# Decoding a weight tile over two attention pairs instead of one

## The chip, the cores and the metric

The kernel runs on one core of one Trainium2 chip. The metric is the device time of one execution in microseconds (us); it is given as the median of several executions. The engines are named as the profile names them: PE (matrix products; PEld is its weight load), DVE (vector), ACT (activation), POOL (GpSimd) and SP (the queue that issues nearly all DMAs).

## The reference

What has to be computed, in float32, cut to what matters:

```python
# q, k, v: (4, 8, 576, 64)
scores = softmax(causal(q @ k.T / 8))          # per batch and head, 576 x 576
local  = scores @ v
q_p    = elu(q) + 1
mem    = (q_p @ M_prev) / (q_p . z_prev + 1e-6)
x      = g * mem + (1 - g) * local             # g = sigmoid(beta), one per head
x      = x.transpose(0, 2, 1, 3).reshape(2304, 512)
h = x @ w_in;  y = (h * tanh(softplus(h))) @ w_out      # 512 -> 2048 -> 512
out = (((y @ w1) * (y @ w2)) @ w3) @ w_out2             # 512 -> 1024 -> 512
```

## The kernel before

The program is written with a tile framework whose planner places the instructions: it simulates the program with estimated costs and gives each engine its queue in the order in which instructions become ready there, the one written first going first. `tc.issue_after(ins)` adds an order against `ins` for the instructions of the block on the same engine only.

**Attention.** There are 16 pairs of heads (NPAIR; a pair is two heads of one batch), worked on one after the other by the loop at lines 578 to 653, with a 17th pass (p = 16) that finishes the last pair and begins the feed-forward part. Pass p loads pair p + 2 (`load_pair`, `load_v`), takes the scores of pair p in blocks of rows, and transposes, multiplies and stores pair p - 1. In the order of the pass:

- `s_blocks(p, (3,))`, `s_blocks(p, (2,))`, `s_blocks(p, (0, 1))` and `s_last(p)`: the score products on PE into a two-bank PSUM tile psA, the row minima of the negated, masked scores on DVE (`maxed`, L400; the text calls them the maxima, as the names do), the exponentials on ACT (L405). Blocks 0 and 1 are the small blocks. `taken[0]` is the last L400 so far.
- `pt_g(p - 1, ..)`: transposes of pair p - 1's weights on PE (L66) into psF, copied out on ACT (L457).
- `prep(p + 1, ..)`: transposes of the next q and k (L66 into psX, copied by ACT, L320), and qd on POOL (L326).
- `normed(p, ..)`: the scaling of the exponentials (L383, L384 on small tiles, then L388 eight times, four on DVE and four on POOL).
- `pv(p - 1)`: the products with v and the memory (psX and psF), copied as a high part by ACT (L478) and a low part by DVE (`sub`, L79). `split_x[0]` is the last such L79.
- `phi_terms(p + 1)`: L342 on ACT, L343 and L349 on POOL, L344 on DVE; `phi_norm(p)`: L358 to L361 on DVE, L364 on POOL.

psX and psF have two banks each, used in turn. A bank is taken again when its reader is through: the first transposes of a pass (`pt_g(p - 1, 1)`) take the psF bank that L79 of the last `pv` reads.

**Decoding.** Each weight is stored as 64-bit words. A tile of 128 x 512 words is fetched by one DMA of 512 KB (`fetch`, L131, tile draw), decoded by six DVE operations (L110, L111, L114, L117, L120, L121) and a POOL addition (L125) into the tile da, and then split into a high part (L76, POOL) and a low part (L79, POOL) in wqt. All six DVE operations and the three of POOL are over 128 x 512 elements.

Eight tiles, the first quarter of w_in and w_out (`load_quarter(0)`: four of w_in, then four of w_out), are decoded during attention. `fetch_next()` issues a tile's DMA, `begin()` puts its seven operations (the last holds L125, L76 and L79) into the list `parts`, and `drip(n, behind)` writes the next n of them. Before, one tile takes one pass: with begin at p = 4 to 11, L110, L111 and L114 stand behind the small blocks' maxima of pass p, L117 behind the L79 of `pv(p - 1)`, L120 behind the maxima of block 3 of pass p + 1, and L121 with the three POOL operations behind those of block 2. draw and da have two buffers each.

**After attention** the first half of the feed-forward part begins with `h_steps((0, 0))` inside pass 16, which reads the w_in tiles; `emit_x2((0, 0))` reads the w_out tiles, the last of them in the second half of each of its output blocks. Two further tiles are decoded right after the first `split_y` (`run(pre, 2)`, line 781). At the end of attention its pools are closed, and x2 takes the place of the decoder's tiles.

Of the kernel before, what the change touches and what calls it, by code (L numbers as in the profile page):

```python
# [21 lines left out]
def fused_kernel(ctx: ExitStack, tc, q, k, v, M_prev, z_prev, beta, w_in, w_out, w1, w2, w3, w_out2, out):  # L22
# [45 lines left out]
    def in_turn(fn, *args):  # L68

        if not ordered[0]:  # L70
            return fn(*args)
        with tc.issue_after(tail[0]):
            return fn(*args)
# [23 lines left out]
    def decoder(stack, raw, n, w=WN, side="left"):  # L97
        dec.update(pool=stack.enter_context(tc.tile_pool(name="dec", bufs=1, side=side)), raw=raw, n=n, w=w)
# [104 lines left out]
    def ensure_x(b):  # L203
        if b not in xl:
            xl[b] = xp.tile([128, 2, KD, 2 * S], F32R, tag=f"xs{b}", name=f"xt{b}")
# [17 lines left out]


    at = ExitStack()
    decoder(at, 2, 2)
    ap_ = at.enter_context(tc.tile_pool(name="attn", bufs=1))

    ek = ExitStack()
# [1 line left out]
    NPAIR = B * NP  # L231
# [52 lines left out]
    def load_pair(p):  # L284
        b, c = divmod(p, NP)
        h0 = 2 * c
        t = {}
        for nm, src in (("q", q), ("k", k)):
            a = ep.tile([128, NB, 2, D], F32, tag="qk", name="raw", bufs=4)
            go = nc.scalar.dma_start if p == 0 and nm == "k" else dm  # L290
            for e in range(2):
                go(out=a[:, 0:4, e], in_=src[b, h0 + e, 0:512, :].rearrange("(i p) d -> p i d", p=128))
            go(out=a[:, 4], in_=src[b, h0:h0 + 2, S - 128:S, :].rearrange("h p d -> p h d"))
            t[nm] = a
        st[p] = t

    def load_v(p):
        b, c = divmod(p, NP)
        h0 = 2 * c
        a = ap_.tile([128, NB, 2, D], F32, tag="vr", name="raw", bufs=3)  # L300
        st[p]["z"] = ep.tile([128, 2, D], F32, tag="zr", name="zr", bufs=3)
        dm(out=st[p]["z"], in_=z_prev[b, h0:h0 + 2].partition_broadcast(128))
        for e in range(2):
            dm(out=a[:, 0:4, e], in_=v[b, h0 + e, 0:512, :].rearrange("(i p) d -> p i d", p=128))
        for hv in (UP, DN):
            dm(out=a[hv, 4], in_=v[b, h0:h0 + 2, 512:S, :].rearrange("h p d -> p h d"))
        st[p]["v"] = a
# [69 lines left out]
    def normed(p, xs):  # L377

        d = st[p]
        og = ogp[:, p % NP]  # L380
        sl = slice(0, 8) if len(xs) > 1 else slice(8, 9)
        rv = d["sum"][:, sl]
        nc.vector.tensor_scalar(out=rv, in0=rv, scalar1=1e-9, scalar2=None, op0=ALU.add)  # L383
        nc.vector.reciprocal(out=rv, in_=rv)  # L384
        for ib, e in xs:
            s = s4[:, 0:S] if ib == 4 else d["s"][ib, e]
            x = 8 if ib == 4 else 2 * ib + e
            r = (nc.gpsimd if x in ON_POOL else nc.vector).tensor_scalar(  # L388
                out=s, in0=s, scalar1=d["sum"][:, x:x + 1], scalar2=og[:, x:x + 1], op0=ALU.mult, op1=ALU.mult
            )  # L390
            if x in ON_POOL:
                scaled[0] = r.ins

    taken = [None]
    scaled = [None]
    split_x = [None]
# [86 lines left out]
    def h_steps(u):  # L483

        g, n = u
        t = wts[g]
        x = xl[n // 3]
        cs = slice(CH * (n % 3), CH * (n % 3) + CH)
        y = [wps[0].tile([128, 2, CH], F32, tag=f"y{i}", name="y", bufs=1) for i in range(2)]
        hp = []  # L490
        for m in range(KQ):
            j = m - (u == (0, 1))
            if j < 0:
                o = psX()[:, 0:CH]
            else:
                if j % 2 == 0:
                    two = psA()
                o = two[:, j % 2, 0:CH]
            ms = slice(128 * m, 128 * m + 128)
            for kk in range(KD):  # L500
                mm(o, t[:, 0, kk, ms], x[:, 0, kk, cs], kk == 0, False)
                mm(o, t[:, 0, kk, ms], x[:, 1, kk, cs], False, False)
                mm(o, t[:, 1, kk, ms], x[:, 0, kk, cs], False, kk == KD - 1)
            hp.append(o)
            yield
        for m in range(KQ):
            nc.scalar.activation(out=y[m // 2][:, m % 2], in_=hp[m], func=AF.Tanh, scale=0.5)  # L507

        d = wps[0].tile([128, 1], F32, tag="dum", name="dum", bufs=2)
        with ExitStack() as k_:  # L510
            if u == (0, 0):
                k_.enter_context(tc.issue_after(copied[0]))
            first = nc.scalar.activation(out=d, in_=y[1][:, 1, 0:1], func=AF.Sin, scale=0.0)
        with tc.issue_after(first.ins):
            for i in range(2):
                nc.scalar.activation(out=y[i], in_=y[i], func=AF.Arctan, scale=-0.5, bias=half)
        for i in range(2):
            nc.scalar.activation(out=y[i], in_=y[i], func=AF.Sin, scale=-2.0, bias=halfpi)  # L518
            for j in range(2):
                nc.vector.tensor_tensor(out=y[i][:, j], in0=y[i][:, j], in1=hp[2 * i + j], op=ALU.mult)  # L520
        yield y

    def emit_h(u, beside=iter(())):

        for m, y in enumerate(h_steps(u)):
            if m == 1:
                steps(beside, 1)
        return y
# [27 lines left out]
    def fetch_next():  # L556
        for src, done in islice(lq0, 1):
            ahead.append((fetch(src), done))

    def begin():  # L560
        r, done = ahead.pop(0)
        ops, a, flat = decode_ops(r)

        def last():
            ops[6]()
            done(a, flat)

        parts.extend(ops[0:6] + [last])

    def drip(n, behind):  # L570

        with tc.issue_after(behind):
            for op in parts[:n]:
                op()
        del parts[:n]

    pre = predecode()
    for p in range(NPAIR + 1):

        now, old, new = p < NPAIR, p > 0, p + 1 < NPAIR  # L580
        ordered[0] = True
        if old:
            ensure_x((p - 1) // (2 * NP))
        if not now:
            ek.close()
            wps[0] = wk.enter_context(tc.tile_pool(name="wp", bufs=1, side="right"))
            h0 = h_steps((0, 0))
        if p + 2 < NPAIR:
            load_pair(p + 2)
            load_v(p + 2)  # L590
        if 3 <= p < 11:
            fetch_next()
        if now:
            in_turn(s_blocks, p, (3,))
            drip(1, taken[0])
            if p == 1:
                in_turn(trans_phi, 0)
        else:
            normed(p - 1, [(4, None)])
            in_turn(next, h0)  # L600
        if old:
            in_turn(pt_g, p - 1, 1)
            in_turn(pt_g, p - 1, 0)
            if not now:
                in_turn(next, h0)
        else:
            gate_values(b_)
            phi_terms(0)
            in_turn(prep, 1, "q")
        if now:  # L610
            in_turn(s_blocks, p, (2,))
            drip(2, taken[0])
            with tc.issue_after(taken[0]):
                if old:
                    normed(p - 1, [(4, None)])
                phi_norm(p)
        if old:
            in_turn(pt_g, p - 1, 4)
            in_turn(pt_g, p - 1, 2)
            if not now:  # L620
                in_turn(next, h0)
            if new:
                in_turn(prep, p + 1, "q")
            in_turn(pt_g, p - 1, 3)
            if not now:
                in_turn(next, h0)
        else:
            in_turn(prep, 1, "k")
        if now:
            in_turn(s_blocks, p, (0, 1))  # L630
            if 4 <= p < 12:
                begin()
                drip(3, taken[0])
        if old and new:
            in_turn(prep, p + 1, "k")
        if old:
            in_turn(pt_g, p - 1, 5)
            in_turn(pt_g, p - 1, 6)
        if now:
            in_turn(s_last, p)  # L640
            with tc.issue_after(taken[0]):
                normed(p, [(i, e) for e in range(2) for i in range(4)])
        if old:
            in_turn(pv, p - 1)
            drip(1, split_x[0])
        if not now:
            split = split_y((0, 0), next(h0))
            early = {(0, 1): emit_h((0, 1))}
        if new:
            with tc.issue_after(taken[0]):  # L650
                phi_terms(p + 1)
        if now and p > 0:
            in_turn(trans_phi, p)
# [260 lines left out]
```

## Time and profile before

| what | value |
|---|---|
| median of 3 executions | 1000.93 us (1000.35 to 1000.98) |
| the profiled execution | 1000.65 us |
| its span, first to last instruction | 998.9 us |
| PE busy | 966.7 us (97%) |
| DVE busy | 639.1 us (64%) |
| ACT busy | 498.4 us (50%) |
| POOL busy | 331.1 us (33%) |
| granted clock of PE, mean of the span | 1.000 |

The shares are means over stages with different limits. The attention part takes up to about 249 us from the start; the rest is the feed-forward part. In the rows below times are us from the start of the span unless marked ns. In rows of a timeline the first two numbers are the start and the length; square brackets hold the engine's idle time before the instruction, and what ended it.

### The profile page before, as it was taken

Reading aid. Unit: us, or ns where it says so; the run is one execution under the profiler, and the core shown is the slowest. Engines: PE = TensorE matmul, PEld = TensorE weight load, DVE = VectorE, ACT = ScalarE, POOL = GpSimd, SP = SyncE. Lnnn points to the kernel's source line nnn. Section 1 sums busy time; section 2 is a strip of 40 time slices with the busy share of each in tenths; the row PEclk is TensorE's granted clock in tenths of the full one; section 3 lists DMA queues with packets and bytes.
Section 4 is the critical chain, followed back from the end, with each engine's and each line's share of the span. In section 5 each row is a group of like instructions: output and inputs, shape, how many; then the busy total and the mean of one; then the engine's idle time right before and its main releaser. Section 6 shows DMA issues by size and latency. Waiting matters only on the chain.

```text
span 998.9 us, 15097 instructions
## 1 busy us (share of the span) xinstructions
PE 966.7 (97%) x5584; PEld 823.6 (82%) x5584; DVE 639.1 (64%) x1380; ACT 498.4 (50%) x1016; POOL 331.1 (33%) x329
## 2 busy tenths in 40 slices
PE   6999888899999999999999999999999999999998
PEld 3565555567999999999999999998888888888897
DVE  5789999974669888988988587676752121121111
ACT  6888677786755555555555554451241221221112
POOL 5547666742244545544454221112400000000000
PEclk9999999999999999999999999999999999999999
DMA  7534443301222242324332672252220100100001
GB/s 160 135 74 110 98 119 81 81 16 64 65 98 92 88 157 99 121 87 138 115 111 81 234 259 98 74 169 74 69 79 1 42 1 1 43 1 22 22 1 64
DMA packets 95770, 85.93 MB, mean 86 GB/s; under 512 B 68816, under 2 KB 72912, under 8 KB 95696
## 3 DMA queue, kind: packets, MB, share of 16 engines
q1 hardware_dynamic: 94368, 84.63, 27.4%
q8 instruction: 44, 0.72, 0.3%
q10 hardware_dynamic: 1328, 0.33, 0.2%
q14 instruction: 30, 0.25, 0.1%
HBM read 67.64 MB, written 17.30 MB: 85 GB/s over the span
## 4 chain that ended last, share of the span: by engine, by line
PE 63%; DVE 25%; ACT 6%; issue 2%; DMA 2%; SPq 1%; POOL 1%; ACTq 0%; DVEq 0%; POOLq 0%
PE psA L63 34%; PE psX L63 15%; PE psF L63 12%; DVE da L117 3%; DVE s L400 3%; DVE draw L120 3%; DVE da L111 3%; DVE da L114 2%; DVE s L388 2%; DVE da L110 2%; ACT s L405 2%; DVE y L520 2%; DVE draw L121 2%; PE psF L66 1%; DVE gl L79 1%
## 5 line engine op out<-in xcount | busy, mean ns | idle before, releaser
L63 PE MATMUL psA<-xt,wqt 128*128 128x384 f32 x1140 | 206.3, 336 | 1.4 <-DVE y L520 1.0
L125 POOL TENSOR_TENSOR da<-da,draw 128x512 f32<-128x512 f32 x72 | 99.0, 1381 | 311.9 <-DVE draw L121 231.8
L63 PEld LDWEIGHTS psA<-xt,wqt 128*128 128x128 f32 x1140 | 197.7, 188 | 4.4 <-DVE y L520 3.6
L842 DVE TENSOR_TENSOR bs<-bs,psA 128x512 f32<-128x512 f32 (+1 forms) x40 | 25.3, 633 | 170.2 <-ACT bs L841 170.2
L63 PE MATMUL psX<-gh,wqt 128*128 128x384 f32 x480 | 122.3, 335 | 0.0
L63 PE MATMUL psA<-x2h,w12t 128*128 128x512 f32 (+1 forms) x384 | 105.4, 354 | 0.0
L841 ACT COPY bs<-psA 128x512 f32<-128x512 f32 (+1 forms) x40 | 21.8, 544 | 164.4 <-PE psA L63 161.8
L405 ACT ACTIVATE s<-s,acc 128x512 f32<-128x512 f32 (+2 forms) x144 | 85.6, 600 | 19.8 <-DVE acc L400 19.2
L63 PE MATMUL psA<-x2s,w12t 128*128 128x512 f32 x384 | 89.6, 389 | 0.0
L63 PEld LDWEIGHTS psX<-gh,wqt 128*128 128x128 f32 x480 | 86.8, 188 | 0.7
L63 PEld LDWEIGHTS psA<-x2s,w12t 128*128 128x128 f32 x384 | 72.1, 188 | 15.0
L63 PE MATMUL psX<-gl,wqt 128*128 128x384 f32 x240 | 80.2, 335 | 0.0
L400 DVE CUSTOM_DVE_ANT_0 s<-psA,mask 128x512 f32<-128x512 f32 (+2 forms) x144 | 63.4, 477 | 24.4 <-PE psA L63 24.0
L66 PEld LDWEIGHTS psF<-ident,s 128*128 128x128 f32 x400 | 43.1, 141 | 43.5 <-ACT pt L457 17.4
L507 ACT ACTIVATE y<-psA 128x384 f32<-128x384 f32 x95 | 41.6, 491 | 71.6 <-PE psA L63 71.3
L63 PEld LDWEIGHTS psA<-x2h,w12t 128*128 128x128 f32 x384 | 68.5, 189 | 10.3
L66 PE MATMUL psF<-ident,s 128*128 128x128 f32 x400 | 61.1, 283 | 14.4 <-DVE xt L79 7.6
L520 DVE TENSOR_TENSOR y<-y,psA 128x384 f32<-128x384 f32 x95 | 48.1, 547 | 41.2 <-ACT y L518 41.2
L63 PE MATMUL psF<-gh,wqt 128*128 128x384 f32 x288 | 73.0, 334 | 0.0
L457 ACT COPY pt<-psF 128x512 f32<-128x512 f32 (+1 forms) x112 | 59.4, 543 | 19.8 <-PE psF L66 19.8
L388 POOL TENSOR_SCALAR s<-s,sum,ogp 128x128 f32<-128x128 f32 (+1 forms) x64 | 53.1, 840 | 45.9 <-DVE sum L384 43.9
L63 PE MATMUL psA<-room,w12t 128*128 128x512 f32 (+1 forms) x192 | 67.9, 354 | 0.0
(121 smaller groups left out, 1903.6 us busy)
## 6 DMA issues: line engine op xcount, KB each, us to landing
draw<-in_moe_w_dram SPq DMA_DIRECT2D x32, 512.0 KB, 3.7
draw<-in_moe_w_out_dram SPq DMA_DIRECT2D x24, 512.0 KB, 3.6
draw<-in_moe_w_in_dram SPq DMA_DIRECT2D x16, 512.0 KB, 4.4
out_dram<-ob SPq DMA_DIRECT2D x18, 256.0 KB, 2.0
raw<-in_q_dram SPq DMA_DIRECT2D x32, 128.0 KB, 3.4
raw<-in_v_dram SPq DMA_DIRECT2D x32, 128.0 KB, 2.5
o_dram<-draw SPq DMA_DIRECT2D x8, 512.0 KB, 2.8
w_dram<-draw SPq DMA_DIRECT2D x8, 512.0 KB, 2.8
```

The costliest lines, as they stand in the source:

```text
L63: tail[0] = nc.tensor.matmul(o, lhsT=l, rhs=r, start=start, stop=stop).ins
L66: tail[0] = nc.tensor.transpose(o, src, ident).ins
L111: lambda: V.tensor_scalar(out=a, in0=a, scalar1=2.0 ** -15, scalar2=122879.9921875, op0=ALU.max, op1=ALU.min),
L117: lambda: V.scalar_tensor_tensor(out=ai, in0=hw, scalar=-0x40000000, in1=ai, op0=ALU.bitwise_and, op1=ALU.bitwise_or),
L120: lambda: V.tensor_scalar(out=hw, in0=ai, scalar1=-0x800000, scalar2=None, op0=ALU.bitwise_and),
L125: lambda: nc.gpsimd.tensor_tensor(out=a, in0=a, in1=lw.bitcast(F32), op=ALU.add),
L388: r = (nc.gpsimd if x in ON_POOL else nc.vector).tensor_scalar(out=s, in0=s, scalar1=d["sum"][:, x:x + 1], scalar2=og[:, x:x + 1], op0=ALU ...
L400: taken[0] = nc.vector.tensor_tensor_reduce(out=s, in0=o, in1=m, op0=ALU.add, op1=ALU.min, scale=-scale, scalar=init, accum_out=a,).ins
L405: nc.scalar.activation(out=s, in_=s, func=AF.Exp, scale=-1.0, bias=a, accum_out=r)
L457: copied[0] = nc.scalar.copy(out=t[:, 0:n], in_=o[:, 0:n]).ins
L507: nc.scalar.activation(out=y[m // 2][:, m % 2], in_=hp[m], func=AF.Tanh, scale=0.5)
L520: nc.vector.tensor_tensor(out=y[i][:, j], in0=y[i][:, j], in1=hp[2 * i + j], op=ALU.mult)
```

## The change

The eight tiles are spread over all sixteen pairs, and each takes two passes. Tiles are fetched at even p from 0 to 14 and begun at odd p from 1 to 15. In odd passes L110, L111 and L114 follow the small blocks' maxima, and L117 the L79 of `pv(p - 1)`: the places that these four had before. In even passes L120, L121 and the three POOL operations follow the small blocks' maxima; nothing follows the maxima of blocks 3 and 2 any more. The last tile is begun at p = 15 and ends in pass 16, behind `pv(15)`. da has one buffer in place of two.

```diff
-    decoder(at, 2, 2)
+    decoder(at, 2, 1)
...
-        if 3 <= p < 11:
+        if p % 2 == 0 and p < NPAIR:
             fetch_next()
         if now:
             in_turn(s_blocks, p, (3,))
-            drip(1, taken[0])
...
             in_turn(s_blocks, p, (2,))
-            drip(2, taken[0])
...
             in_turn(s_blocks, p, (0, 1))
-            if 4 <= p < 12:
+            if p % 2 == 1:
                 begin()
-                drip(3, taken[0])
+            drip(3, taken[0])
...
             in_turn(pv, p - 1)
-            drip(1, split_x[0])
+            if p % 2 == 1 or not now:
+                drip(3 if not now else 1, split_x[0])
```

## Rows read from the trace of the kernel before

**Rows 1.** Windows: stretch, us, busy PE, PEld, DVE, ACT, POOL; PE clock, DMA share, GB/s.
```profile
69.69:83.34 13.65, 13.21 (x104) 8.27 (x102) 12.80 (x41) 11.66 (x35) 9.27 (x10) 1.00 0.37 93
83.34:98.78 15.44, 13.49 (x104) 8.24 (x102) 15.27 (x43) 11.62 (x35) 10.60 (x12) 1.00 0.44 96
...
177.26:193.09 15.83, 13.56 (x104) 8.25 (x103) 15.27 (x42) 11.60 (x35) 10.98 (x12) 1.00 0.30 69
...
206.73:220.38 13.65, 13.21 (x104) 8.27 (x103) 10.05 (x36) 11.66 (x35) 6.98 (x8) 1.00 0.11 26
```

**Rows 2.** Waits of PE from 83 to 193 us: total us, times, longest.
```profile
PE psF L66 <- DVE xt L79: 7.6, 7, 1.1
PE psF L66 <- DVE s L388: 3.2, 7, 0.5
```

**Rows 3.** Timeline of DVE in the frame at 206.73, which has no decoding.
```profile
207.88 0.82 DVE L344 SCALAR_TENSOR_TENSOR phie<-phie,phit 128x640 f32<-128x640 f32 x1
...
209.05 1.45 DVE L388 TENSOR_SCALAR s<-s,sum,ogp 128x256 f32<-128x256 f32 x4
...
211.33 0.21 DVE L79 TENSOR_TENSOR xt<-psF,xt 128x64 fp32r<-128x64 f32 x1
...
220.58 0.46 DVE L400 CUSTOM_DVE_ANT_0 s<-psA,mask 128x288 f32<-128x288 f32 x1 [1.61 <-PE psA L63]
```

**Rows 4.** Timeline of DVE around 69.69: the first tile, begun in pass 4.
```profile
68.19 0.53 DVE L110 TENSOR_SCALAR da<-draw 128x512 int32<-128x512 int32 x1
...
69.89 0.46 DVE L400 CUSTOM_DVE_ANT_0 s<-psA,mask 128x288 f32<-128x288 f32 x1
...
74.42 0.68 DVE L117 SCALAR_TENSOR_TENSOR da<-draw,da 128x512 int32<-128x512 int32 x1
75.52 0.69 DVE L400 CUSTOM_DVE_ANT_0 s<-psA,mask 128x512 f32<-128x512 f32 x1 [0.41 <-PE psA L63]
```

**Rows 5.** Timelines of POOL and DVE in a later pass with decoding.
```profile
129.34 1.25 POOL L364 TENSOR_TENSOR phie<-phie,dn 128x640 f32<-128x640 f32 x1
...
129.66 1.22 DVE L110 TENSOR_SCALAR da<-draw 128x512 int32<-128x512 int32 x1
```

**Rows 6.** Tile draw up to 240 us: ns shortest/median/longest, first and last start; landing.
```profile
L120 DVE TENSOR_SCALAR draw<-da x8: 801/1300/1680, 76.7 to 185.8; 128x512 int32<-128x512 int32 x8
L121 DVE SCALAR_TENSOR_TENSOR draw<-draw x8: 677/682/690, 78.4 to 188.4; 128x512 f32<-128x512 uint32 x8
...
DMA to landing us min/median/max: 3.5/4.1/6.7
```

**Rows 7.** Tile da over the whole span, its POOL operations: ns shortest/median/longest.
```profile
L125 POOL TENSOR_TENSOR da<-da,draw x72: 1283/1313/1699, 79.2 to 719.5; 128x512 f32<-128x512 f32 x72
...
L76 POOL TENSOR_SCALAR wqt<-da x32: 612/653/829, 81.1 to 551.0; 128x512 fp32r<-128x512 f32 x32
L79 POOL TENSOR_TENSOR wqt<-da,wqt x32: 1277/1312/1453, 83.6 to 551.8; 128x512 fp32r<-128x512 f32 x32
```

**Rows 8.** Timelines of POOL and DVE after the last tile's L121, frame at 193.09.
```profile
193.52 1.28 POOL L79 TENSOR_TENSOR wqt<-da,wqt 128x512 fp32r<-128x512 f32 x1
...
194.23 1.25 DVE L344 SCALAR_TENSOR_TENSOR phie<-phie,phit 128x640 f32<-128x640 f32 x1
...
197.80 0.21 DVE L79 TENSOR_TENSOR xt<-psF,xt 128x64 fp32r<-128x64 f32 x1
```

**Rows 9.** Timeline of PE in the frame at 206.73: the first transposes.
```profile
212.44 1.09 PE L66 MATMUL psF<-ident,s 128*128 128x128 f32 x8
```

**Rows 10.** Timeline of SP near the start: the first load of pair 3.
```profile
19.70 1.09 SPq L292 DMA_DIRECT2D raw<-in_q_dram  x2
```

**Rows 11.** Timelines of DVE and PE after pv(15), as the feed-forward part begins.
```profile
257.42 0.22 DVE L79 TENSOR_TENSOR xt<-psF,xt 128x64 fp32r<-128x64 f32 x1
...
263.15 0.51 PE L63 MATMUL psX<-gh,wqt 128*128 128x384 f32 x2
```

**Rows 12.** Groups of POOL from 60 to 200 us by form: count, busy us, mean ns.
```profile
L388 POOL TENSOR_SCALAR s<-s,sum,ogp 128x512 f32<-128x512 f32 x20 | 20.1, 1003 | 0.0
```

## The prediction

> **What bounds the kernel now.** I read the windows first, cut into frames: a frame runs from the first `pv` product of one pair to that of the next, so that one frame is one pass of the loop, and t is the time from a frame's start. What follows the small blocks' maxima of a pass lies at the end of a frame (t from 12.2), and goes on in the next. A plain frame takes 13.65 us, with PE busy for 13.21 and DVE for 10.05. The seven frames from 83.34 to 193.09 take 15.4 to 15.8, and there DVE is busy for 15.27 of 15.44 and PE waits [rows 1]. So a pair alone is bound by PE, and a pair with a whole tile by DVE. Second, the waits of PE in these seven frames: 7.6 us for the L79 that gives back a psF bank, once in each frame, and 3.2 for an L388 [rows 2]. Seven plain frames would take 95.5 us; these take 193.09 - 83.34 = 109.75. **14.2 us** is thus all that decoding costs in attention. After attention the change touches nothing but the last tile.
>
> Third, the timelines, to see why 10.05 us of plain work and a tile make 15.3. L110 takes 0.53 us in pass 4 [rows 4] and 1.22 in a later one [rows 5]: there it starts 0.32 us after POOL's L364 and ends 0.29 us after it, so most of its length is waiting for POOL. L120 likewise has 0.80 to 1.68 us [rows 6]. A tile costs DVE more than its own work because its operations lie beside POOL's.
>
> Here the Trainium skill bears ("SBUF — State Buffer", Who interferes with whom): a DVE instruction that uses the port pair it shares with GpSimd, and a GpSimd instruction, exclude one another, and whichever issued first holds the pair for its whole length. [Rows 5] agree with it: L110 goes on to 0.29 us past the end of L364. It speaks against this change, which puts three POOL operations just ahead of four such DVE instructions. By the rule the time is that of the forecast or, in its strictest reading, of rival 3; without it, that of rival 1.
>
> **What goes.** L120 and L121 with the POOL operations leave the middle of the pass, and no pass holds a whole tile any more. If all frames become plain, 14.2 us go. Below this I see nothing to gain: in a plain frame PE is busy for all but 0.44 us.
>
> **Odd passes: L110, L111, L114, then L117.** These keep their places, and the trace has the case: pass 4 began the first tile with no tile before it. L110 starts at 68.19, and the minima of `s_last` behind the three start at 69.89 [rows 4]. In the plain frame they start at 220.58, after 1.61 us of idle DVE, which is t = 13.85; 69.89 is t = 13.85 of the frame from 56.04 [rows 1, 3, 4]. The idle time takes all three and none is left over. L117 takes 0.68 at 74.42 and DVE still waits 0.41 us for PE behind it [rows 4]. The frame from 69.69, with L117, a L120 and a L121 in it, takes 13.65 [rows 1]. Price: 0. Without that cover the three would cost up to 1.6 us a pass. Pass 15 has less idle time before its `s_last`, but there PE has `h_steps` between; I take 0.
>
> **Even passes: L120, L121, then L125, L76, L79.** In passes 2 to 14 L120 stands where L110 stood in pass 4, so 0.53 us from t = 12.15 [rows 4]; L121 has 0.68 [rows 6], and a little more if it meets POOL's L326. Both end at about t = 13.55, before `s_last` at 13.85: no loss on DVE so far. Then POOL starts: L125 1.28, L76 0.65, L79 1.31 [rows 7]. In the next frame's t, L125 runs from about -0.05 to 1.24. What meets it is the phi step and the scaling. In the plain frame L344 starts at t = 1.15, the four L388 at 2.32 and end at 3.77, and the last L79 of DVE ends at 4.81; the transposes that take its psF bank start at 5.71 [rows 3, 9]: 0.90 us of cover. With the three, each operation going when the one that was there first has ended:
> - L344 follows L125 and has 0.8 [rows 3]: 1.2 to 2.0. It waits little.
> - L76 has waited and goes next, to 2.65. L383 waits for it, and it and L384 take the 0.35 that lie between L344 and L388 in the plain frame [rows 3]: to 3.0.
> - L79 on POOL has started at 2.65 and runs to 3.95. The first of the four L388 on DVE waits for that: 3.95 instead of 2.32.
> - The four L388 take 1.45 as before, to 5.4. The two L79 of DVE end 1.04 after them in the plain frame, in part because ACT's copy comes late; here it has been made, so some 0.8: to 6.2. The transposes start then, instead of at 5.71.
>
> This gives **0.5 us** of PE time in each of seven frames, 3.5 in all; I count on none of the 0.44 us that PE idles in a plain frame to take it up. The bounds: 0 if L383 and the L388s slip in ahead of POOL's L79. The nearest row speaks for a low price: in the frame at 193.09 POOL's L79 ran at 193.52, L344 took 1.25 instead of 0.82, and the last L79 of DVE still ended at t = 4.92, in a frame of plain length [rows 1, 8]; but there only one POOL operation was left over, not three. Above: 0.9 a frame, if POOL's own four L388, now some 1.5 us later, hold up the transposes that read them too. I take 0.5.
>
> **The last tile.** In pass 16 L120, L121 and the three follow the L79 at 257.42. DVE ends 1.0 us later, POOL's 3.25 us then end near 261.9. The first output block of `emit_x2((0, 0))` reads the tile's part from 263.15 [rows 11]. That covers it with 1.2 us; two tiles that DVE decodes beside it make POOL slower (L79 up to 1.45, L76 up to 0.83 [rows 7]). I take 0.2; bounds 0 and 2.
>
> **Transfers and the single da.** SP issues the first tile before the loads of pair 3, which start at 19.70 [rows 10]; with the longest landing of 6.7 us [rows 6] it is there at 26.4, and L110 of pass 1 comes 1.5 us ahead of the frame at 28.75 (three plain frames before 69.69), near 27.2. Cost 0; if the planner puts it 5 us later, DVE and `s_last` of pass 1 wait once, up to 3 us. A later fetch takes the draw buffer that L125 of the tile two before gave back in the pass before, so it need not wait; if the planner puts it earlier in SP's queue, loads of v or of q and k stand behind its wait, and they have a pass to spare. da is written again at the end of the odd pass, 8 us after POOL's L79 read it: its one buffer costs nothing.
>
> **Sum.** Against the profiled execution: 1000.65 - 14.2 + 3.5 + 0.2 = 990.15. The median lies 0.28 above the profiled one: **990.4 us**.
>
> **Rivals.**
> 1. *POOL hides wholly*: L383 and the L388s run before POOL's L79 or beside it. All frames are plain: 1000.93 - 14.2 = 986.7 us. For it: rows 8. Against: there the L79 was nearly through when the scaling began.
> 2. *More is lost than the one bank*: L388 of POOL ends late, transposes wait for that as well, 0.9 to 1.3 us a frame: 993.2 to 996 us.
> 3. *Slower*: the two engines take strict turns, and not only with the tile's operations. After L79 (t = 3.95) each of DVE's four L388 would let one of POOL's through; that adds three turns, of which one is 1.0 us [rows 12] and the others shorter, some 2.0 in all. The last L79 would end at 8.2 and PE lose 2.5 us a frame: 1000.93 - 14.2 + 17.5 + 0.2 = 1004.4 us. It decides from 14.2 / 7 = 2.03 us a frame. Against it: in the plain frames DVE's four L388 take the same 1.45 us though POOL's four lie beside them.
> 4. *The planner does something else*: it places operations by planned times and not where they are written, so that L120 and L121 or the POOL operations land ahead of other work and a third to all of the 14.2 us stays: 995 to 1001 us.
>
> **How the numbers follow.** Forecast (988 to 992.5) 0.45; rival 1 0.2; rival 2 0.15; rival 3 0.06; rival 4 0.14, a third of it within 0.2% of now. A measurement of this kernel can tell some 0.2% from no change, 2 us. Faster: 0.45 + 0.2 + 0.15 + 0.09 = 0.89; same 0.04; slower 0.07. The range runs from rival 1, 986.3 with the spread of the runs, to 995.0, which holds most of rival 2 and leaves out rivals 3 and 4.
>
> **What would show it.** Right: the frames after the start are all 13.6 to 14.2 long, even passes followed by the longer ones; DVE is busy for 12 to 13.5 us in each, L110 near 0.53 and never 1.2; PE's waits for DVE's L79 fall from 7.6 us to about 3.5; attention ends 10 to 11 us earlier and the rest has its old length. Wrong: L388 on DVE that take over 2 us for the four, PE waits of over 2 us in frames behind even passes, a wait of L110 for its DMA in pass 1, or of PE for wqt near the start of the feed-forward part.

## The result and the profile after

| what | before | after |
|---|---|---|
| median, executions side by side on one chip | 1000.95 us (1000.35 to 1001.33) | 990.12 us (989.36 to 990.67) |
| the profiled execution | 1000.65 us | 989.59 us |
| its span | 998.9 us | 987.8 us |

The ratio is 0.9892, with an interval of 0.9875 to 0.9909. The forecast was 990.4 us. The sum came out, but two of its terms were wrong, in opposite directions. Line numbers of after are those of before up to 590 and one lower from 645 on.

The windows of after, cut into frames as in [rows 1]: stretch, us, busy PE, PEld, DVE, ACT, POOL; clock, DMA share, GB/s. The first is a frame behind an odd pass, the second one behind an even pass, the third is all of attention's frames, the last what comes behind the first product of pv(15).

```profile
82.96:96.60 13.64, 13.20 (x103) 8.26 (x102) 12.02 (x40) 11.66 (x35) 7.71 (x9) 1.00 0.32 71
96.60:110.31 13.71, 13.27 (x103) 8.27 (x102) 12.52 (x39) 11.66 (x35) 10.66 (x11) 1.00 0.49 122
28.25:234.50 206.25, 199.87 (x1540) 128.24 (x1539) 176.12 (x563) 169.31 (x491) 130.65 (x135) 1.00 0.38 91
234.50:987.80 753.30, 745.51 (x3948) 683.73 (x3946) 439.84 (x752) 310.45 (x471) 191.64 (x163) 1.00 0.24 83
```

The same two stretches of before, from its first product of pv(0) at 28.75 and from that of pv(15) at 248.82:

```profile
28.75:248.82 220.07, 201.61 (x1539) 128.12 (x1538) 186.92 (x567) 168.71 (x491) 131.10 (x138) 1.00 0.35 85
248.82:998.90 750.08, 744.95 (x3948) 683.82 (x3946) 436.20 (x750) 310.35 (x471) 183.27 (x160) 1.00 0.24 83
```

The span is shorter by 11.10 us: 0.50 at the start (28.75 to 28.25; this differs from run to run of one kernel), **13.82 in the frames** (220.07 - 206.25), and **3.22 given back** behind them (753.30 - 750.08). The frames of 15.4 to 15.8 us [rows 1] are gone; the full frames of attention are plain, or 0.06 us above it behind an even pass. DVE's busy time in attention fell by 10.8 us (186.92 to 176.12); the last tile's L120 and L121, 1.1 us, now lie behind it.

The waits of PE in attention (28.7 to 232 us): total us, times, longest.

```profile
PE psX L66 <- ACT qt L320: 5.1, 13, 0.4
PE psF L66 <- ACT pt L457: 0.5, 1, 0.5
```

Neither line of [rows 2] is left: PE waits for no L79 and no L388.

Timelines of DVE in an even pass and the frame behind it (the frame starts at 123.95), then of POOL and PE:

```profile
122.46 0.53 DVE L120 TENSOR_SCALAR draw<-da 128x512 int32<-128x512 int32 x1
123.03 0.82 DVE L121 SCALAR_TENSOR_TENSOR draw<-draw 128x512 f32<-128x512 uint32 x1
...
125.10 0.82 DVE L344 SCALAR_TENSOR_TENSOR phie<-phie,phit 128x640 f32<-128x640 f32 x1
125.84 0.58 DVE L383 TENSOR_SCALAR sum<-sum 128x8 f32<-128x8 f32 x1
...
126.69 2.25 DVE L388 TENSOR_SCALAR s<-s,sum,ogp 128x256 f32<-128x256 f32 x4
...
129.46 0.21 DVE L79 TENSOR_TENSOR xt<-psF,xt 128x64 fp32r<-128x64 f32 x1
```

```profile
123.93 1.29 POOL L125 TENSOR_TENSOR da<-da,draw 128x512 f32<-128x512 f32 x1 [0.63 <-DVE draw L121]
125.31 1.08 POOL L76 TENSOR_SCALAR wqt<-da 128x512 fp32r<-128x512 f32 x1
126.48 1.27 POOL L79 TENSOR_TENSOR wqt<-da,wqt 128x512 fp32r<-128x512 f32 x1
127.74 2.96 POOL L388 TENSOR_SCALAR s<-s,sum,ogp 128x128 f32<-128x128 f32 x4
```

```profile
129.72 1.09 PE L66 MATMUL psF<-ident,s 128*128 128x128 f32 x8
```

The operations come in the predicted order. L344 ends behind L125, L76 behind L344 (1.08 us where [rows 7] have 0.65), and the four L388 meet POOL's L79 and take 2.25 instead of 1.45 [rows 3]. The last L79 ends at 129.67, t = 5.72, and the transposes start at 129.72, t = 5.77, against 5.71 in the plain frame. The cover is used up: the bank comes back 0.01 us later than the plain frame's transposes start.

The beginning of the feed-forward part: DVE, POOL and PE of after.

```profile
243.09 0.21 DVE L79 TENSOR_TENSOR xt<-psF,xt 128x64 fp32r<-128x64 f32 x1
243.22 0.41 DVE L120 TENSOR_SCALAR draw<-da 128x512 int32<-128x512 int32 x1
243.55 0.95 DVE L79 TENSOR_TENSOR gl<-y,gh 128x768 fp32r<-128x768 f32 x1
244.42 0.75 DVE L110 TENSOR_SCALAR da<-draw 128x512 int32<-128x512 int32 x2
245.09 0.68 DVE L121 SCALAR_TENSOR_TENSOR draw<-draw 128x512 f32<-128x512 uint32 x1
245.69 0.75 DVE L111 TENSOR_SCALAR da<-da 128x512 f32<-128x512 f32 x2
246.37 0.75 DVE L114 TENSOR_SCALAR da<-da 128x512 int32<-128x512 int32 x2
247.04 1.29 DVE L117 SCALAR_TENSOR_TENSOR da<-draw,da 128x512 int32<-128x512 int32 x2
248.24 0.76 DVE L120 TENSOR_SCALAR draw<-da 128x512 int32<-128x512 int32 x2
248.91 1.29 DVE L121 SCALAR_TENSOR_TENSOR draw<-draw 128x512 f32<-128x512 uint32 x2
```

```profile
245.86 5.48 POOL L125 TENSOR_TENSOR da<-da,draw 128x512 f32<-128x512 f32 x1 [21.38 <-DVE draw L121]
251.44 0.62 POOL L76 TENSOR_SCALAR wqt<-da 128x512 fp32r<-128x512 f32 x1
```

```profile
249.86 0.51 PE L63 MATMUL psF<-gh,wqt 128*128 128x384 f32 x2
252.11 0.44 PE L63 MATMUL psX<-gh,wqt 128*128 128x384 f32 x1 [1.73 <-POOL wqt L76]
```

The single L120 at 243.22 and L121 at 245.09 are the last tile's; the planner put the L79 of gl and the two L110 between them. From 244.42 on the other rows of DVE are the two tiles of `run(pre, 2)`; all of it goes on without a gap to 250.20. L125 of the last tile took 5.48 us, and PE then waited 1.73 us for the L76 behind it. L125's own length is 1.28 [rows 7]; 251.34 - 1.28 = 250.06, so it did its work when DVE's train was as good as through.

### The profile page after: what moved, and what is told of

It is laid out like the page before. It is cut to its first block, busy times and chain, and to the rows that moved or that the text cites. A ratio compares the mean times of both kernels' runs of the same rounds, so it can differ in the third digit from the quotient of the medians.

```text
span 987.8 us, 15111 instructions
## 1 busy us (share of the span) xinstructions
PE 964.8 (98%) x5584; PEld 823.5 (83%) x5584; DVE 633.3 (64%) x1380; ACT 499.0 (51%) x1016; POOL 339.2 (34%) x329
## 4 chain that ended last, share of the span: by engine, by line
PE 65%; DVE 14%; ACT 10%; issue 4%; DMA 3%; POOL 2%; SPq 1%; ACTq 0%; POOLq 0%; DVEq 0%
PE psA L63 33%; PE psX L63 16%; PE psF L63 12%; ACT s L405 4%; DVE da L117 2%; PE psF L66 2%; ACT pt L457 2%; DVE da L114 2%; DVE y L520 2%; DVE draw L120 2%; PE psX L66 2%; DVE da L111 1%; DMA draw<-in_moe_w_dram 1%; DVE gl L79 1%; DVE draw L121 1%
## 5 line engine op out<-in xcount | busy, mean ns | idle before, releaser
L125 POOL TENSOR_TENSOR da<-da,draw 128x512 f32<-128x512 f32 x72 | 103.0, 1435 | 294.8 <-DVE draw L121 221.1
L535 ACT CAST gh<-y 128x768 fp32r<-128x768 f32 x48 | 40.2, 837 | 55.2 <-DVE y L520 24.1
```

What stands on the lines that cost most here:

```text
L125: lambda: nc.gpsimd.tensor_tensor(out=a, in0=a, in1=lw.bitcast(F32), op=ALU.add),
L535: nc.scalar.copy(out=gh, in_=y[i])
```

## The experiments

The theory: the frames keep the whole gain because the even passes just fit into the cover of [rows 9], spreading the tiles is what makes them plain, and some 2 us are lost where the last tile's L125 meets the two tiles of `run(pre, 2)`. The rivals: the loss has another cause (the later w_out tile, the start of the feed-forward part); the new places and not the spreading bring the gain; the POOL operations cost nothing for another reason than the cover.

**The last tile done early.** The last tile's L117 is followed in pass 15 by its other operations, and pass 16 has none. The kernel ran twice, the second time beside the kernel after.

```diff
-            if p % 2 == 1 or not now:
-                drip(3 if not now else 1, split_x[0])
+            if p % 2 == 1:
+                drip(4 if p == NPAIR - 1 else 1, split_x[0])
```

> The changed kernel, but the last tile's L117, L120, L121 and its three POOL operations all follow the L79 of pv(14) in pass 15, and nothing of it is left for pass 16. In the changed kernel the part from pv(15) on takes 753.3 us against 750.1 before, L125 of the last tile takes 5.48 us there, and PE waits for wqt. Theory A: the 3.2 us are this tile, caught on POOL beside two tiles that DVE decodes. Then the part is back at 750.1 us, no PE wait for wqt is left, and the median is 990.1 - 3.2 = 986.9 us. Rival B: the 3.2 us come from elsewhere (the place of x2, the new order of the queues). Then 989.5 to 990.5 us.

> The changed kernel once more, beside the others of this series on one chip. 989.4 to 990.7 us as before, or the same distance of some 11 us to the kernel before.

> The kernel of e1_last_early once more, beside the changed kernel on one chip. Theory A (the last tile costs 2 to 3 us in pass 16): 1.5 to 3 us under f0_after. Rival B: within 0.5 us of it.

The first run gave 988.18 us (987.94 to 988.21), 0.986 of before. That is 1.3 us more than the 986.9 expected: the part from pv(15) on takes 751.60 us, not 750.08. Most of what is left there is a wait at the first w3 tile, on which the last run bears. Side by side, the kernel after gave 991.52 (990.72 to 991.95) and the early one 988.38 (987.88 to 989.54): 3.14 us less. The timeline of POOL, of the first run, has L125 of the last tile at its plain length, and PE waits for no wqt:

```profile
226.61 1.31 POOL L125 TENSOR_TENSOR da<-da,draw 128x512 f32<-128x512 f32 x1 [1.81 <-DVE draw L121]
```

The loss belongs to the last tile's place in pass 16, and it is larger than PE's wait. In the profile of after that was run here, PE's timeline shows why:

```profile
252.69 0.44 PE L63 MATMUL psX<-gh,wqt 128*128 128x384 f32 x1 [1.76 <-POOL wqt L76]
...
255.05 0.52 PE L63 MATMUL psX<-gh,wqt 128*128 128x384 f32 x1
...
258.53 0.33 PE L63 MATMUL psX<-gl,wqt 128*128 128x384 f32 x1
```

Behind the wait PE runs more slowly until about 256: matmuls of one shape have 0.52 us and then 0.33. The windows of this run give a granted clock of 0.65 from 252 to 256, a mean between its two levels (1.2 and 2.4 GHz); in the first profile of after the same stretch, behind a wait of 1.73, has 1.00:

```profile
252.00:256.00 4.00, 3.31 (x11) 3.31 (x12) 1.97 (x5) 1.33 (x2) 3.90 (x4) 0.65 0.00 0
```

```profile
252.00:256.00 4.00, 3.89 (x22) 3.87 (x23) 3.21 (x7) 0.78 (x1) 3.92 (x5) 1.00 0.00 0
```

The first profile loses 2.03 us at this point and this one 3.57. The run with two da buffers (below), which has the last tile in the same place, waits 1.8, loses 2.05 and keeps 1.00. Why the clock fell in one run and not in the others is not settled.

**The two tiles of `run(pre, 2)` moved away.** The last tile stays in pass 16; the two tiles are decoded later.

```diff
             if n == 0 and not last:
-                run(pre, 2)
+                if u != (0, 0):
+                    run(pre, 2)
...
+            if u == (0, 3):
+                run(pre, 2)
```

> The changed kernel with the last tile in pass 16 as it is, but without the two further tiles that DVE decodes right beside it: they are decoded 3 feed-forward steps later. Theory A (DVE's back-to-back operations keep POOL's L125 from its operands, 5.48 us for 1.3): L125 of the last tile takes 1.3 to 1.5 us, PE has no wait for wqt, and the part after pv(15) begins without the loss of 2.0 us within its first 28 us. Rival B (the tile is merely begun too late, or x2 waits): PE still waits 1 to 2 us near t = 15 after pv(15). The whole time is no test, since the two tiles now crowd a later step.

The timeline of POOL:

```profile
247.06 1.29 POOL L125 TENSOR_TENSOR da<-da,draw 128x512 f32<-128x512 f32 x1 [20.70 <-DVE draw L121]
```

L125 takes 1.29 instead of 5.48, and nothing is lost in the first 60 us behind pv(15). So the train of DVE operations kept it waiting, and not its pass or its tile. The whole time, 1006.36 us, says nothing on this, since the two tiles crowd the steps that they were moved to.

**POOL's L79 doubled.** On top of the early last tile, each of the eight tiles has its low part computed and written a second time, with the same values.

```diff
+            if again:
+                sub(lo, a, hi, nc.gpsimd)
```

> As e1_last_early, but POOL's L79 is done twice for each of the eight tiles decoded in attention (the same result is written again). It lengthens what POOL does behind an even pass's small blocks by 1.27 us. Theory A: the three POOL operations hide just within the cover (the last L79 of DVE ends at t = 5.72, where the transposes want its bank at 5.71, and POOL's second L388 ends 0.6 us ahead of its reader), so a fourth is paid: some 1.0 to 1.5 us in each of seven frames, 7 to 10 us over e1_last_early, and PE waits for L388 or L79. Rival B: POOL has reserve and DVE goes first whenever it wants to: 0 to 1 us over e1_last_early.

988.61 us (988.05 to 988.68), against 988.18 without it: no difference clear of the spread. But the planner had not left the second L79 behind the first. It stands behind L349 (L351 here), after DVE's L388 and L79:

```profile
130.91 1.55 POOL L351 TENSOR_TENSOR qz<-phie,zr 128x640 f32<-128x640 f32 x1
132.41 1.28 POOL L79 TENSOR_TENSOR wqt<-da,wqt 128x512 fp32r<-128x512 f32 x1
```

So this tells nothing of the cover. It was run again with an order for POOL: its L388 of even passes are held behind the second L79.

```diff
             with tc.issue_after(taken[0]), ExitStack() as k_:
+                if second[0] is not None and p % 2 == 0:
+                    k_.enter_context(tc.issue_after(second[0]))
```

> As e1_last_early, with POOL's L79 done twice for each tile decoded in attention, and with the scaling that follows on POOL (its four L388) held behind the second one, since the planner put the second L79 of e3_sub_twice behind L349, where POOL had nothing to do. Theory A (the train of POOL operations fits its cover to within 0.1 us on DVE's side and 0.6 us on POOL's): frames behind even passes take 14.4 to 15.2 us, seven of them 5 to 10 us more than e1_last_early, and PE waits for an L388 of POOL or for L79. Rival B (POOL's end is not awaited): frames stay at 13.7 us and the time within 1 us of e1_last_early.

995.17 us (994.57 to 996.92), 6.8 above the early kernel on the same chip. A frame behind an even pass and one behind an odd pass in the windows; POOL, DVE and PE in the timelines; the waits of PE:

```profile
100.50:115.23 14.73, 13.26 (x103) 8.26 (x102) 13.46 (x39) 11.67 (x35) 11.78 (x12) 1.00 0.45 112
115.23:128.88 13.65, 13.20 (x103) 8.27 (x102) 12.01 (x40) 11.77 (x35) 7.72 (x9) 1.00 0.35 80
```

```profile
103.02 2.62 POOL L79 TENSOR_TENSOR wqt<-da,wqt 128x512 fp32r<-128x512 f32 x2
```

```profile
103.24 3.27 DVE L392 TENSOR_SCALAR s<-s,sum,ogp 128x256 f32<-128x256 f32 x4
```

```profile
107.29 1.09 PE L66 MATMUL psF<-ident,s 128*128 128x128 f32 x8 [1.02 <-DVE xt L79]
```

```profile
PE psF L66 <- DVE xt L79: 7.1, 7, 1.0
```

(L392 here is L388 of after.) One further POOL operation of 1.27 us costs 1.02 to 1.03 us in each of seven frames. DVE's L388 wait for POOL, the L79 behind them gives its bank back late, and PE waits. That is the chain of the prediction, with its price: of 1.27 us beyond the cover 1.02 are paid, and the kernel after stands at its edge.

**Spreading alone.** Two passes to a tile, but the six operations of DVE in the places that they had before (L120 behind the maxima of block 3, L121 and the three behind those of block 2); the last tile early. It ran twice.

```diff
             in_turn(s_blocks, p, (3,))
+            if p % 2 == 0:
+                drip(1, taken[0])
...
             in_turn(s_blocks, p, (2,))
+            if p % 2 == 0:
+                drip(2, taken[0])
...
             if p % 2 == 1:
                 begin()
-            drip(3, taken[0])
+                drip(3, taken[0])
```

> As e1_last_early (eight tiles over sixteen pairs, one da), but in even passes L120 stands behind block 3's maxima and L121 with the POOL operations behind block 2's, as before the change. It is the spreading alone. Theory A: what the change gives is the spreading, no pass holding more DVE work than PE's 13.65 us; all frames are 13.6 to 13.7 us, within 0.5 us of e1_last_early. Rival B: it is the new places; then frames behind even passes stay 0.5 to 2 us too long, 3.5 to 14 us over e1_last_early.

> The kernel of e5_old_places once more, beside e4_two_da on one chip: frames of 13.65 us without exception, and 3 to 4.5 us under e4_two_da (the last tile's 2 to 3.6 us, and 0.06 us in each of seven frames).

986.99 us (986.74 to 988.70), ratio 0.9853 (0.9834 to 0.9872), and 987.54 (986.57 to 988.92), ratio 0.9868 (0.9854 to 0.9883). These are the lowest medians of all. On the chip of the first run this kernel lies 1.2 us under the early kernel, where at most 0.5 were expected and the frames give 0.4; its four executions lie 2 us apart, so the rest is open. Two frames of the second run, behind an odd and an even pass, and POOL around them:

```profile
96.98:110.62 13.64, 13.20 (x103) 8.26 (x102) 11.60 (x39) 11.65 (x35) 8.64 (x10) 1.00 0.49 109
110.62:124.27 13.65, 13.21 (x104) 8.26 (x102) 12.19 (x40) 11.76 (x35) 9.26 (x10) 1.00 0.34 90
```

```profile
120.11 1.29 POOL L125 TENSOR_TENSOR da<-da,draw 128x512 f32<-128x512 f32 x1 [1.92 <-DVE sum L383]
...
122.07 0.81 POOL L76 TENSOR_SCALAR wqt<-da 128x512 fp32r<-128x512 f32 x1
```

Every full frame is plain. With half a tile to a pass the old places cost nothing, and the new ones bring nothing beside them.

**New places alone.** One tile to a pass as before (fetched from p = 3, begun at 4 to 11), with L120, L121 and the three behind the small blocks' maxima of the next pass, ahead of the next tile's first three; two da buffers. The edit is against the kernel before.

```diff
             in_turn(s_blocks, p, (3,))
-            drip(1, taken[0])
...
             in_turn(s_blocks, p, (2,))
-            drip(2, taken[0])
...
             in_turn(s_blocks, p, (0, 1))
+            drip(3, taken[0])
             if 4 <= p < 12:
                 begin()
```

> Eight tiles in passes 4 to 11, one to a pass, with two da, as before the change, but in the new places: L120, L121 and the POOL operations of one tile behind the small blocks' maxima, then L110, L111 and L114 of the next. It is the new places alone. Theory A (spreading is what counts): five operations of 2.9 us stand in 1.6 us of idle time, each such frame takes 14.6 to 15.7 us, and the median is 994 to 1001 us. Rival B (the places count): 986.5 to 990 us.

993.63 us (992.99 to 994.36), ratio 0.9916 (0.9898 to 0.9933). Two of its frames, and the waits:

```profile
99.09:113.27 14.18, 13.27 (x103) 8.26 (x102) 13.87 (x43) 11.75 (x35) 11.52 (x11) 1.00 0.46 115
113.27:127.67 14.40, 13.27 (x103) 8.27 (x102) 14.10 (x43) 11.79 (x35) 11.53 (x11) 1.00 0.43 111
```

```profile
PE psF L66 <- DVE xt L79: 4.2, 7, 0.7
```

The places bring more than the theory allowed (frames of 14.6 us and over, 994 us and over), if a whole tile has to go into one pass: frames of 14.18 to 14.57 instead of 15.4 to 15.8. The eight frames that hold tiles lie 5.3 us above plain ones in all, where before the seven lay 14.2 above. DVE is still the bound, with 14.10 of 14.40 us busy. On this chip the places alone gain 8.4 us by the medians (1002.02 - 993.63), spreading alone 15.0. Spreading reaches plain frames by itself, so it is the larger cause, and the places are one that is no longer needed.

**Two da buffers.** The kernel after with `decoder(at, 2, 2)`.

> The changed kernel with two da in place of one. Theory A (da is written again 8 us after its last reader, one buffer costs nothing): the same frames to 0.02 us and a time within 0.7 us of the changed kernel's 990 to 991.5 us. Rival B (the single da holds L110 up or moves the layout): 1 us or more apart.

990.77 us (990.0 to 993.13), ratio 0.9897 (0.988 to 0.9913), against 0.9892 and 0.9898 of the kernel after, with frames of the same lengths. The single buffer costs nothing that can be measured.

**The kernel before once more,** for the part behind attention.

> The kernel before once more, for its profile alone. In all profiles with spread tiles PE waits some 1.0 us for L125 of the first w3 tile near t = 335 after pv(15), which the first profile of the kernel before does not show. If this is of the change, it is absent here again; if it varies from run to run or chip to chip, it may be here.

1002.05 us. Of the 3.22 us that after gives back, 2.03 lie at the wait for the last tile. A further 1.0 come at the first w3 tile, some 335 us behind pv(15), where PE waits for its L125. That same wait is in this profile of before (first line; the second is after, whose L707 is L708 of before), and the part from pv(15) on takes 751.67 us here, not 750.08:

```profile
PE psF L708 <- POOL da L125: 1.1, 1, 1.1
```

```profile
PE psF L707 <- POOL da L125: 0.7, 1, 0.7
```

It comes and goes from run to run: one of the two profiles of before has it, and all but one of the eleven others. So it does not need the change; whether the change makes it more frequent, two profiles of before cannot tell.

## Why the prediction was right, step by step

**What bounds the kernel before: right.** A pair alone is bound by PE, a pair with a whole tile by DVE. 14.2 us was put down as all that decoding costs in attention; the spread tiles in their old places give plain frames and gain 13.3 to 15.0 us (1000.88 - 987.54 and 1002.02 - 986.99, medians on one chip).

**Odd passes, price 0: right.** Frames behind them take 13.64 to 13.65. The rows of tile draw up to 226 us, to be held against [rows 5, 6]: ns shortest, median, longest.

```profile
L110 DVE TENSOR_SCALAR da<-draw x8: 428/530/539, 26.7 to 218.2; 128x512 int32<-128x512 int32 x8
```

L110 was predicted near 0.53 and never at 1.2; it is 0.54 at most. It still meets L364, but only its end: at the end of one frame L364 runs from 107.79 to 109.05 and L110 from 108.81 to 109.34, 0.24 us together, where in [rows 5] L110 stands beside L364 for 0.93. POOL reaches L364 earlier, since L125 and L76 no longer lie ahead of it in the pass.

**Even passes, 0.5 us a frame: the mechanism right, the size wrong.** Measured is 0.06 a frame, 0.4 in all against 3.5. The predicted t of each end stands against the timeline above (less 123.95): L344 2.0 and 1.97, L384 3.0 and 2.70, POOL's L79 3.95 and 3.80, the last L388 5.4 and 4.99, DVE's last L79 6.2 and 5.72. The 0.48 us between the last two are three small terms that were all rounded up: POOL's L79 ended 0.15 earlier, the L388s ended 1.19 and not 1.45 us behind it, and the two L79 of DVE took 0.73 and not 0.8. The 1.45 is the step that failed most: it is the length of the four from the first one's start, but the first one's record begins at 126.69, while POOL's L79 still runs, so that a part of its own length lies before the end of the wait: alone it takes 0.41 us, and here it ends 0.15 behind POOL's L79. Against a cover of 0.90 us, a delay of 0.91 costs nearly nothing and one of 1.39 costs 0.5, so that errors of a few tenths in a chain of five decide the term. The lower bound of 0 held, and the row that was named as nearest, the frame at 193.09 [rows 8], had the better value.

**The last tile, 0.2 us with bounds of 0 and 2: wrong.** It costs 2.03 us in one profile, 3.57 in another, and 3.14 between medians. Two steps failed. The smaller is DVE's "1.0 us later": L121 ends 2.5 us behind the end of that L79 (243.30 to 245.77), since an L79 of 0.95 us and the two L110 came before it, so that L125 became ready inside the train. The larger is POOL's 3.25 us, which two tiles beside it were to "make slower" only a little: lengths up to 1.45 for L79 and 0.83 for L76 [rows 7] were taken as what DVE can do to POOL. The longest L125 of before has 1.70 us [rows 7], so none of those had waited for a whole train of DVE operations. Here two tiles were decoded without a gap for some 4.5 us (245.69 to 250.20), and L125 waited through all of it. The code showed the train (`run(pre, 2)` writes 12 DVE operations in a row); no row of before showed a POOL operation ready beside it, because before the last tile was through by then. The upper bound should have come from the length of that train: 4.5 us less the 1.2 us of cover are 3.3, and a fall of PE's clock behind the wait comes on top. The wait itself was shorter, 1.73 us: PE took products of the next output block first and wanted the tile only at 250.38, where the 263.15 of the prediction stands for 248.83 here, and it wanted no more than L76's part.

**Transfers and the single da, 0: right.** The first tile's L110 starts at 26.7 (predicted 27.2). The two buffers gave the same time.

**The sum.** 1000.65 - 14.2 + 0.4 + 2.0 gives 988.85; the varying wait at the first w3 tile (1.0), the start (-0.5) and a rest of 0.15 that no row explains bring it to 989.5, beside 989.59 measured. That the forecast of 990.15 for this execution came so close is luck: 3.1 us too much in one place stood against 1.8 too little in the other, and the varying 1.0 and -0.5 were in no term. Of the rivals the first, in which POOL's operations hide wholly, describes the frames almost exactly, though not by its mechanism: L383 and the L388s did not run ahead of POOL's L79, and DVE waited as in the forecast. Rivals 2 and 4 did not come. Rival 3 did not come either, but the doubled L79 shows its mechanism: in the single records behind that row, DVE's first L388 ends 0.15 us behind the first of POOL's L79 and the second 0.21 behind the second, so that the engines did take turns there. Beside POOL's L388s, DVE's other two ran at their own lengths, 0.34 and 0.47.

**The signs.** The frames and DVE's 12.02 and 12.52 us a frame came as named. PE's waits for DVE's L79 fell to none and not to 3.5 us, and attention ended 14.3 us earlier (248.82 to 234.50), not 10 to 11, with a longer rest. Two of the signs of being wrong came as well: the four L388 took 2.25 us, because the first one's wait for POOL's L79 lies inside its record, and PE waited for wqt as the feed-forward part began, which is the last tile's term.

## What to carry to other kernels

First ask how much of a helper's work a stage can hold: here spreading eight tiles over all sixteen pairs made every frame plain by itself in the old places, and to within 0.06 us in the new ones. A POOL operation whose result is waited for should not become ready beside a long unbroken train of DVE operations: here its wait had nearly the train's length, not that of the longest of its kind seen so far. Where a chain ends within a few tenths of its cover, measure the cover by lengthening the chain: here one more operation of 1.27 us cost 1.02.

## What the runs showed of the hardware

- One POOL addition waited 4.2 us (5.48 instead of 1.28) behind ten DVE operations that followed one another without a gap, and took 1.29 us once the train was moved away. By the Trainium skill ("SBUF — State Buffer", Who interferes with whom) the instruction issued first holds the shared pair for its whole length, and the other one is blocked. The trace goes beyond that: L125's record starts at 245.86, while the first of the ten runs, the other nine start behind it, and the pair did not pass to it between them.
- In the other direction, two POOL operations in a row did let one DVE operation through between them (the doubled L79).
- A wait of PE of 1.76 us was followed by about 3 us in which the granted clock was lower in one profile (a mean of 0.65 from 252 to 256), while one of 1.73 in the same place was followed by 1.00 in another.
